# Reordering three transposes in an attention kernel: late queries, extra keys by way of the segment's key buffer, normed rows ahead of the extra keys

## Chip, cores and metric

One core of one Trainium2 chip. The metric is the device time of the core in microseconds (us), lower is better.

## What is computed

The input is 2048 tokens of 640 elements. `x` is normed and goes through attention in 64 segments of 32 tokens; each segment carries 8 memory rows that are the output of the segment before. So the segments are strictly one after the other. A ReLU-gated feed-forward block follows.

```python
# cut: B=1, S=2048, D=640, H=32 heads of 128, M=8 memory rows, seg=32, F=1728
def _A_ref(x, mem0, Wq, Wk, Wv, Wo, seg_len):
    mem = mem0
    for s in range(n_seg):
        xs = x[:, s * seg_len:(s + 1) * seg_len, :]
        h = jnp.concatenate([mem, xs], axis=1)          # 40 rows
        q, k, v = (einsum('btd,dhe->bhte', h, W) for W in (Wq, Wk, Wv))
        p = softmax(where(mask, q @ k.T * scale, -1e9))
        o = einsum('bhte,hed->btd', p @ v, Wo)
        mem = o[:, :M, :]
        outs.append(o[:, M:, :])
h  = x + _A_ref(layernorm(x), ...)
h2 = h + (relu(gate) * up) @ W_down                     # of layernorm(h)
```

## The kernel before

TensorE projects keys, then queries, then values. A segment's projection has 32 columns of room and only 8 memory rows, so 24 tokens of coming segments ride along ("riders"); every four segments the 32 tokens that are left over ("extra") are projected as filler work. I number the four kinds of segment by `s % 4`. Kind 2 does the extra keys and scales the normed rows of the next block; kind 3 follows it. In four later blocks (`EARLY`) kind 0 also scales rows, for the second norm.

Keys and queries must be transposed. They leave TensorE's output banks into four token buffers `tok` (0 and 1 keys, 2 and 3 queries). From there a DMA transpose, always issued by SyncE (SP), takes them to `KS` (keys), `QS` (queries) or, for the extra keys, straight to `Kr`. The normed rows go by the same queue from `xt` to `at`.

```python
    def dma_t(dst, src, r, w):
        add("sp", lambda e: e.dma_start_transpose(dst, src), r=r, w=w, dma=True)

    def trans_q(after=()):                       # QS <- tok[2], tok[3]
        dma_t(QS..., tokp[1][:, :], [("tok", 2), ("tok", 3)] + list(after), [("QS",)])
```

Every operation names what it reads (`r`) and writes (`w`). From these the program derives the waits: whoever overwrites a buffer waits until its readers are done. For a DMA "done" means landed. The wait stands in the queue of the engine that issues; SP works through its queue in order, so one wait of SP holds up all transposes behind it.

The loop, cut to what the change touches:

```python
        # ... keys of segment s projected into BQ
        dma_t(KS..., tokp[0][:, :], [("tok", 0), ("tok", 1)], [("KS",)])
        trans_ox()                               # oT <- ox, same queue
        # ... queries projected, copied to tok[2], tok[3]
        for f in late_k + late_q:
            f()
        qlate = nr and s % 4 < 2
        if nr and not qlate and s < NSEG - 2:
            trans_q()                            # kinds 2 and 3: at once
        loads()
        # ... values projected; pick_mem reads tok[2], tok[3] (L453)
        scores(s)                                # reads KS, Kr, Qr (L572)
        exp_mem()
        # ...
        if nr:
            v_riders(t0, nr, ...)                # small stores into Vr
            if s < NSEG - 2 and not qlate:
                evac_q(QS, ("QS",), t0, nr, M, "act")
        # ... filler work, memory values, mask
        n = n_rows(nb) if s % 4 == 2 and ln else 128 if e2b is not None else 0
        if n:
            row_scale(xt, ("xt",), n, xt, ("xt",))
        filler(4)
        if evac:
            evac()          # kind 2: tok[2], tok[3] <- BQ, then Kr <- tok
        # ... output projection
        if qlate and s < NSEG - 2:
            trans_q(...)                         # kinds 0 and 1: late
            late_k.append(... evac_q ...)
        pv_x(s, P0)                              # L690
        if n:
            dma_t(chunks_of(at[:, :])[:, :, 0:n], xt[0:n, :], [("xt",)], [("at",)])
```

The softmax here doesn't subtract the row's maximum and nothing guards it: scores larger than these inputs give would overflow.

## Time and profile before

| what | before |
|---|---|
| time | 1097.09 us, median of 3 runs (1093.23 to 1100.27) |
| span of the profiled run, granted clock | 1095.7 us, 0.997 |
| mean length of a segment, kinds 0, 1, 2, 3 | 13.28, 13.57, 13.67, 13.63 us |
| scores waiting for KS, all segments | 1.6 us in 5 waits |

A segment is measured from the end of the last product with the segment's own values (L690) to the end of the next one.

### The profile page before, as it was taken

How to read it: one execution, taken by the hardware profiler on the slowest of the kernel's cores; microseconds unless marked ns; L12 is line 12 of the kernel's file. 1: busy time of each engine (PE TensorE's matmuls, PEld its weight loads, DVE VectorE, ACT ScalarE, POOL GpSimd, SP SyncE). 2: the span in 40 equal slices, each digit the busy share in tenths (PEclk: the TensorE clock that was granted, in tenths of full speed). 3: DMA queues.
4: the chain of work that ended last, by engine and by line, in shares of the span. 5: the costliest groups of instructions: out<-in, count | busy, mean ns of one | idle time of the engine just before them, and what ended most of it. 6: DMA issues, size and time to landing. Idle time of an engine off the chain costs nothing.

```text
span 1095.7 us, 55782 instructions
## 1 busy us (share of the span) xinstructions
PE 1054.8 (96%) x27875; PEld 517.3 (47%) x23292; DVE 608.8 (56%) x1673; ACT 362.6 (33%) x792; POOL 260.0 (24%) x521
## 2 busy tenths in 40 slices
PE   4689999999999999999999999999999999999999
PEld 2344545454545454544454544454545465444444
DVE  3245656565656565666666666565656554553532
ACT  1214343333333333333333333333333322231211
POOL 1013232323223232323232323232323243000000
PEclk9999999999999999999999999999999999999999
DMA  9946464546454654556566666554555448122100
GB/s 363 387 101 106 89 107 90 102 89 104 90 98 95 102 94 97 94 114 108 112 113 112 110 109 109 100 97 95 95 94 93 92 118 288 45 78 74 29 19 25
DMA packets 285371, 121.61 MB, mean 111 GB/s; under 512 B 260880, under 2 KB 274788, under 8 KB 285136
## 3 DMA queue, kind: packets, MB, share of 16 engines
q1 hardware_dynamic: 267456, 95.52, 41.9%
q0 software_dynamic: 17264, 22.26, 8.8%
q8 instruction: 201, 3.29, 1.3%
q14 instruction: 34, 0.28, 0.1%
q10 hardware_dynamic: 416, 0.26, 0.1%
HBM read 36.79 MB, written 7.19 MB: 40 GB/s over the span
## 4 chain that ended last, share of the span: by engine, by line
PE 91%; DMA 5%; SPq 3%; DVE 1%; issue 1%; ACT 0%; DVEq 0%
PE ps L422 25%; PE ps L400 24%; PE ps L644 13%; PE ps L1051 11%; PE ps L690 3%; PE ps L666 3%; PE ps L572 3%; SPq L360 3%; DMA Wo<-in_A_Wo_dram 3%; PE ps L1092 3%; PE ps L609 2%; DMA KS<-tok 2%; PE ps L453 2%; PE ps L624 1%; DMA Kr<-tok 1%
## 5 line engine op out<-in xcount | busy, mean ns | idle before, releaser
L422 PE MATMUL ps<-W,act_r 128*32 128x512 bf16 x4292 | 406.5, 384 | 6.8 <-DMA W<-in_A_Wv_dram 2.6
L400 PE MATMUL ps<-W,act_r 128*32 128x512 bf16 x3588 | 362.4, 379 | 0.0
L422 PEld LDWEIGHTS ps<-W,act_r 128*32 128x32 bf16 x4292 | 132.1, 97 | 250.4 <-issue 151.3
L360 POOL DMA_DIRECT2D Vr<-Vp x312 | 156.1, 508 | 345.9 <-ACT Px L591 274.0
L464 ACT ACTIVATE tok<-ps 128x512 bf16<-128x512 f32 x192 | 110.9, 593 | 229.0 <-PE ps L400 200.2
L644 PE MATMUL ps<-Wo,oT 128*32 128x160 bf16 x8064 | 156.9, 234 | 8.7 <-DMA Wo<-in_A_Wo_dram 4.8
L466 DVE CAST tok<-ps 128x512 bf16<-128x512 f32 x131 | 90.6, 691 | 129.6 <-PE ps L400 109.8
L644 PEld LDWEIGHTS ps<-Wo,oT 128*32 128x32 bf16 x8064 | 142.8, 97 | 30.3 <-DVE oT L466 16.2
L422 PE MATMUL ps<-W,act_e 128*32 128x512 bf16 x900 | 89.3, 381 | 0.0
L400 PE MATMUL ps<-W,act_e 128*32 128x512 bf16 x900 | 88.9, 379 | 0.0
L555 DVE STREAM_TRANSPOSE TBf<-ps 128x64 f32<-128x64 f32 (+1 forms) x128 | 33.6, 263 | 95.8 <-PE ps L644 95.7
L360 POOL DMA_DIRECT2D attn_d<-wtok x62 | 46.4, 748 | 161.0 <-ACT wtok L464 161.0
L705 DVE TENSOR_TENSOR ox<-ps,rx 128x512 bf16<-128x512 f32 x128 | 82.5, 686 | 2.2
L464 ACT ACTIVATE Qr<-QS 128x512 bf16<-128x512 bf16 (+3 forms) x107 | 69.7, 680 | 35.9 <-DMA QS<-tok 35.9
L464 ACT ACTIVATE Vp<-ps 128x256 bf16<-128x256 f32 (+1 forms) x126 | 48.5, 385 | 81.5 <-PE ps L400 79.0
L1066 DVE TENSOR_TENSOR hT<-g,ps 128x512 bf16<-128x512 bf16 (+1 forms) x56 | 38.5, 688 | 47.2 <-PE ps L1051 43.4
L1051 PE MATMUL ps<-xn2T,Wg 128*128 128x512 bf16 x260 | 64.6, 379 | 0.0
L1051 PE MATMUL ps<-xn2T,Wu 128*128 128x512 bf16 x260 | 64.6, 379 | 0.0
L1064 ACT ACTIVATE g<-ps 128x512 bf16<-128x512 f32 (+1 forms) x56 | 32.4, 592 | 91.6 <-PE ps L1051 91.6
L466 DVE CAST Vp<-ps 128x512 bf16<-128x512 f32 x64 | 44.2, 691 | 28.4 <-PE ps L400 22.9
L464 ACT ACTIVATE wtok<-ps 128x160 bf16<-128x160 f32 x62 | 18.8, 303 | 117.0 <-DVE TBf L555 117.0
L1092 PE MATMUL ps<-Wd,hT 128*128 128x320 bf16 x210 | 57.2, 299 | 0.0
(121 smaller groups left out, 1190.7 us busy)
## 6 DMA issues: line engine op xcount, KB each, us to landing
Vr<-Vp POOLq DMA_DIRECT2D x124, 48.8 KB, 2.0
W<-in_A_Wk_dram SPq DMA_DIRECT2D x2, 2560.0 KB, 13.4
W<-in_A_Wq_dram SPq DMA_DIRECT2D x2, 2560.0 KB, 23.1
W<-in_A_Wv_dram SPq DMA_DIRECT2D x2, 2560.0 KB, 27.7
Wo<-in_A_Wo_dram SPq DMA_DIRECT2D x2, 2560.0 KB, 28.5
xt<-in_A_x_dram SPq DMA_DIRECT2D x30, 160.0 KB, 2.7
Vr<-Vp POOLq DMA_DIRECT2D x96, 32.5 KB, 2.1
at<-attn_d SPq DMA_DIRECT2D x16, 160.0 KB, 3.7
```

Of the source, the lines that this page charges most:

```text
L360: add(eng, lambda e: e.dma_start(dst, src), r=r, w=w, dma=True)
L400: return pe.add_instruction(mybir.InstMatmult(name=nc.get_next_instruction_name(), engine=mybir.EngineType.PE, ins=[pe.lower_ap(rhs), pe.l ...
L422: ins = pe.matmul(*a, start=(c == 0), stop=(c == DC - 1), skip_group_check=True)
L464: add("act", lambda a: a.activation(dst, src, ACTF.Copy), r=r, w=w)
L466: add("dve", lambda v: v.tensor_copy(dst, src), r=r, w=w)
L555: add("dve", lambda v, lo=lo, hi=hi: v.transpose(TBf[:, lo:hi, :].rearrange("p c t -> p (c t)"), src[:, 32 * lo:32 * hi]), r=[wkey], w=[(" ...
L572: i = pe.matmul(bank((P0, P1)[g % 2])[p:p + (M if a else 32), 40 * k:40 * k + 40], lh, Qr[:, h, q, :], start=True, stop=True, skip_group_c ...
L644: i = pe.matmul(bank(bk)[32 * gg:32 * gg + 32, 0:160], src[:, hb, :], w[:, gg], start=(hb == ORDER[0]), stop=(hb == ORDER[31]), skip_group ...
L705: add("dve", lambda v, kh=kh: v.tensor_tensor(ox[:, :, kh, :], src[:, :, kh, 0:128], ap(rx, kh, [[2, 4], [0, 128]]), ALU.mult), r=[B(b0 + ...
L1051: ins = pe.matmul(bank(bk), w[:, c, lo:lo + 128], xn2T[par][:, :, c, :], start=(c == 0), stop=(c == DC - 1))
L1066: add("dve", lambda v: v.tensor_tensor(hT[par][lo:128, j, :], g1[gi][lo:128, :], bank(bu)[lo:128, :], ALU.mult), r=[B(bu), ("g1", gi)], w= ...
L1092: i = pe.matmul(*a, start=(j == 0), stop=(j == FC - 1), skip_group_check=True)
```

## The change

Three parts, which I call A, B and C.

- **A, late queries:** in kind 2 the query transpose is issued after the memory mask, not right after the queries' copies, and its result is copied out in the next segment.
- **B, keys through KS:** the extra keys' tokens are copied into KS, which the scores have read by then, and Kr is transposed from KS. So `tok[2]` and `tok[3]` are free for the next segment at once.
- **C, rows first:** the normed rows' transpose is issued as soon as the rows are scaled, so that it stands ahead of Kr in SP's queue in kind 2, and ahead of the late query transpose in the four kind-0 segments.

```diff
@@ exp_mem @@                                                   # A
-                r=[("om",), ("mbd",)], w=[("Pbd", i)])
+                r=[("om",), ("mbd",)], w=[("Pbd", i), ("qgo", i)])
@@ extra_units / evac @@                                        # B
+                elif j == 1:
+                    copy_op(e, KS[:]...[:, 512 * i:512 * i + 512], bank(BQ[i]), [B(BQ[i])], [("KS",)])
                 else:
                     to_tok(BQ[i], 2 + i, e)
             if j == 1:
-                dma_t(Kr[q]..., tokp[1][:, :], [("tok", 2), ("tok", 3)], [("Kr", q)])
+                dma_t(Kr[q]..., KS[:]..., [("KS",)], [("Kr", q)])
@@ loop @@                                                      # A
-            if nr and not qlate and s < NSEG - 2:
+            qmid = nr and s % 4 == 2 and s < NSEG - 2
+            if nr and not qlate and not qmid and s < NSEG - 2:
                 trans_q()
@@                                                              # A
-                if s < NSEG - 2 and not qlate:
+                if qmid:
+                    trans_q([("qgo", 1)])
+                if s < NSEG - 2 and not qlate and not qmid:
                     evac_q(QS, ("QS",), t0, nr, M, "act")
@@                                                              # C
             row_scale(xt, ("xt",), n, xt, ("xt",))
+            dma_t(chunks_of(at[:, :])[:, :, 0:n], xt[0:n, :], [("xt",)], [("at",)])
@@                                                              # A
+            if s > 0 and qmid:
+                late_k.append(lambda t0=t0, nr=nr: evac_q(QS, ("QS",), t0, nr, M, "act"))
@@                                                              # C
         pv_x(s, P0)
         if n:
-            dma_t(chunks_of(at[:, :])[:, :, 0:n], xt[0:n, :], [("xt",)], [("at",)])
```

(Cuts: the views of KS and Kr are written as `...`.) No matrix product is added, removed or moved: TensorE's instructions stand in the same order in both kernels.

More of the change, by code (lines that the diff above doesn't have):

```diff
@@ L877, in evac @@
                     to_v(BQ[i], Vr[q], i, ("Vr", q), e)
+                elif j == 1:
+                    copy_op(e, KS[:].rearrange("p h t -> p (h t)")[:, 512 * i:512 * i + 512], bank(BQ[i]), [B(BQ[i])], [("KS",)])
                 else:
@@ L880, in evac @@
             if j == 1:
-                dma_t(Kr[q][:].rearrange("p h t -> p (h t)").rearrange("p (k r) -> p k r", r=128), tokp[1][:, :],
-                      [("tok", 2), ("tok", 3)], [("Kr", q)])
+                dma_t(Kr[q][:].rearrange("p h t -> p (h t)").rearrange("p (k r) -> p k r", r=128),
+                      KS[:].rearrange("p h t -> p (h t)"), [("KS",)], [("Kr", q)])
         def fin():
```

## The prediction

> **What bounds the kernel now.** I read the page first, then the waits, the stretches segment by segment, and last the queue of SyncE (SP) beside TensorE.
>
> From the page: busy time, then the chain that ended last.
>
> ```profile
> PE 1054.8 (96%) x27875; PEld 517.3 (47%) x23292; DVE 608.8 (56%) x1673; ACT 362.6 (33%) x792; POOL 260.0 (24%) x521
> ...
> PE 91%; DMA 5%; SPq 3%; DVE 1%; issue 1%; ACT 0%; DVEq 0%
> ```
>
> TensorE is occupied for 1054.8 of 1095.7 us. Of the missing 41 us, some 30 lie at the start, where the weights arrive (the chain has Wo<-in_A_Wo_dram and SPq L360 there). So the 63 segments between 60.8 and 908 us hold the whole prize of this change, and TensorE hardly stands still in them. The change touches no matrix product; it can only win what separates a disturbed segment from an undisturbed one.
>
> Next, the stretches, each from the end of one segment's last matmuls (L690) to the next one's. I call the four kinds of segment by their number modulo 4. Columns: length, then busy time per engine.
>
> ```profile
> 586.90:600.22 13.32, 13.32 (x414) 6.64 (x334) 9.40 (x27) 5.45 (x12) 2.73 (x5) 1.00 0.55 86
> 600.22:614.29 14.07, 13.68 (x438) 7.16 (x383) 8.07 (x25) 4.09 (x9) 2.74 (x5) 1.00 0.68 112
> 614.29:627.62 13.33, 13.33 (x422) 6.71 (x340) 8.98 (x27) 6.04 (x15) 5.92 (x11) 1.00 0.52 103
> 627.62:642.10 14.48, 13.54 (x420) 6.02 (x340) 7.62 (x22) 4.85 (x10) 4.26 (x10) 1.00 0.99 137
> ```
>
> These are kinds 0, 1, 2, 3. Over the whole loop kind 0 has a median of 13.23 us and kind 1 of 13.30 us, which I take as the undisturbed length of any kind. Summed over the loop (leaving out the second segment and the last full one, which have no filler work) the excess over 13.23 (13.30 in kind 1) is 0.8 us in kind 0, 3.2 in kind 1, 5.1 in kind 2, 6.0 in kind 3: about 15 us, 1.4% of the run. That is the ceiling.
>
> The queue of SP in the disturbed segments, and what TensorE says there:
>
> ```profile
> 601.46 1.29 SPq L363 DMA_TRANSPOSE at<-xt  x1
> 603.31 2.47 SPq L363 DMA_TRANSPOSE KS<-tok  x1
> ...
> 626.47 2.25 SPq L363 DMA_TRANSPOSE Kr<-tok  x1
> 629.17 1.21 SPq L363 DMA_TRANSPOSE at<-xt  x1
> 630.71 2.50 SPq L363 DMA_TRANSPOSE KS<-tok  x1
> ```
> ```profile
> 607.62 0.20 PE L572 MATMUL ps<-Qr,Kr 128*32 128x40 bf16 x4 [0.34 <-DMA KS<-tok]
> ...
> 633.84 0.36 PE L453 MATMUL ps<-ident,tok 128*128 128x32 bf16 x8 [0.87 <-DVE tok L466]
> ```
>
> The first pair: the normed rows' transpose (at<-xt) is issued 1.85 us ahead of the segment's keys (KS<-tok), whose issue then takes 2.47 us; undisturbed it takes 1.23 to 1.8. The keys land late and the scores (L572) stand 0.34 us. The second: VectorE could not overwrite tok because the extra keys' transpose (Kr<-tok) still read it, and TensorE stood 0.87 us. These are the two waits that the diff aims at. The landing times from the list of transfers:
>
> ```profile
> QS<-tok SPq DMA_TRANSPOSE x76, 3.1
> KS<-tok SPq DMA_TRANSPOSE x62, 3.2
> ...
> at<-xt SPq DMA_TRANSPOSE x19, 4.9
> Kr<-tok SPq DMA_TRANSPOSE x15, 5.2
> ```
>
> A transpose alone lands 3.1 us after its issue; at and Kr, issued back to back beside the value riders' stores, need 4.9 and 5.2.
>
> **What the Trainium skill says.** "DMA: Bandwidth & Descriptors", section "Issuing engines are not separate DMA queues": transfers started by different engines run on the same 16 DMA engines and interleave. The trace agrees, with those 5.2 us against 3.1. "Perfetto Trace Analysis", section "DMA Instruction — HWDGE (DVE, Sync)": what the profile shows of such a DMA begins when its semaphores are satisfied and ends when the sequencer is free; the movement lies outside. So 2.47 us for KS is issuing alone. This agrees with a landing (3.1) well beyond the issue (1.25). "Runtime: NRT & Kernel Launch", section "Instruction fetch mechanics": instructions are refilled in 16 KiB blocks of 256. Here the instruction queue q8 shows 201 packets and 3.29 MB, 16 KiB each, and TensorE has 51,167 recorded instructions, 200 blocks of 256. So these fetches share the DMA engines with the transposes, and a transfer that is moved can change stops that seem to have no releaser.
>
> **Part 1: normed rows first.** For kind 2 and four of kind 0, the at transpose is issued once VectorE has scaled the rows, not after the last matmuls are set up. In the kind-2 segment from 396.88 us, row scaling (L383) starts 11.28 us in and takes 0.44, so at can go out at 11.75; today Kr goes at 11.7 and at at 13.05 or, in about half the segments, 0.5 to 1.5 us into kind 3. In the four kind-0 segments scaling ends near 11.5, and at gets out ahead of the late query transpose at 13.2. That frees kind 1 of the pile-up: the four scores waits there are 0.16, 0.22, 0.35 and 0.56 us, 1.3 us in sum. The same four segments are 2.8 us too long in all; I count half of the rest as following from it. **Gain 2.0 us.**
>
> **Part 2: extra keys through KS.** The two ScalarE copies (0.6 us each) stay, only their target changes from tok to KS; no instruction is added. The tok wait vanishes: 0.87 us once, and about 0.5 us in the first kind-3 segment, which reached L453 at 5.79 us and not 5.28. **Gain 1.4 us.** The price: two new waits. The copies overwrite KS, which the scores have long read, but the graph also makes the store of the extra memory rows (attn_d<-at, 3.7 us to landing, issued at 7.0 and 7.6 us) a reader of KS, so the copies start near 11.3 us, not 10.55. Since at goes first in SP's queue until 13.0, this hides. Second, the next segment's KS transpose must wait until Kr has landed. Kr, issued near 13.0 and landing 4 us later, is done at 17.0, which is 3.5 us into kind 3, where KS is issued at 3.1 to 3.25 now. KS then issues fast, because at is no longer in front of it: 3.5 + 3.1 = 6.6 us, against scores at 6.9. Some segments will miss this by a few tenths. **Loss 1.0 us**: 14 segments, an average of 0.07.
>
> **Part 3: late queries in kind 2.** The QS transpose moves from 6.15 us to after the memory mask (L585), near 8.6 us, and its evacuation on ScalarE (0.63 + 0.40 us) to the next segment, after the token copy at 5.3 us: done at 6.3, with the scores at 6.9 and the next value copy at 7.2. So it just fits. It takes away QS traffic while exp and mask run: where QS landed at 9.2 us, the memory's value products (L609) started 1.05 us after the scores' last matmuls were issued; elsewhere, and in kinds 0 and 1, 0.92. That is 0.13 us in 12 segments, 1.5 us; I take 1.0, because the traffic is only moved, into the output projection (L644), where instruction fetches run. **Gain 1.0 us.**
>
> Sum: 2.0 + 1.4 - 1.0 + 1.0 = 3.4 us off 1097.1, which gives 1093.7.
>
> **Rivals.** (a) *The new KS wait takes the place of the tok wait.* If Kr lands at 18 us and not at 17, KS is issued 1.2 us late in all 14 kind-3 segments and the scores stand some 0.8 us each: 11 us lost, net 1105. For it: Kr is now second of two transposes and lands 5.2 us after issue today. Against it: the two together land at 16.7 to 17.5 us now in either order, and with QS gone from 6 us the memory rows' store should land sooner. (b) *The stops without a releaser move.* Kinds 2 and 3 lose up to 0.9 us in the output projection with no data wait, and kind 0 almost never. If they come from fetches behind transposes, three transposes in a row from 8.6 to 15 us may make each kind 2 longer by 0.3 us: 4.5 us lost, net 1098. Or taking at out of kind 3's beginning may remove them: some 5 us more won, net 1088. (c) *Nothing.* The waits that the diff removes sum to under 3 us of TensorE's time and everything else is hidden: 1095 to 1097.
>
> **Range and chances.** The three runs of before span 1093.2 to 1100.3, so plus or minus 3.5 us is noise between runs. With rival (b) both ways, 8 times in 10 the time should be between 1087.5 and 1100. Faster by over 2% needs 22 us, more than the ceiling of 15: 0.01. Slower by over 2% needs rival (a) at twice its size: 0.03. Within 2%: 0.96.
>
> **What would show each step.** Right: no KS wait over 0.1 us in kind 1; no wait of L453 for tok; kind 1's mean at 13.30; KS issued between 3.1 and 3.8 us in kind 3 and scores reached by 7.1; QS issued near 8.6 us in kind 2 with 0.92 us from the scores to L609. Wrong: KS in kind 3 issued after 4 us with the scores waiting for it (rival a), output projections of kind 2 longer than 2.5 us (rival b), or ScalarE's evacuation of QS holding up the scores in kind 3. The whole prediction falls if time moves outside the segment loop, which no part of the change touches.

## More of the kernel before

One view that the prediction does not show is the list of waits. Its columns: who waited `<-` for whom, us in total, number of waits, longest wait. For the scores in the kernel before it says:

```profile
PE ps L572 <- DMA KS<-tok: 1.6, 5, 0.6
```

So scores hardly ever wait for the keys' transpose.

## The result

| | before | after |
|---|---|---|
| median of 4 runs | 1095.91 us (1093.23 to 1100.27) | 1125.61 us (1120.17 to 1130.68) |
| span of the profiled run, granted clock | 1095.7 us, 0.997 | 1124.0 us, 0.992 |
| mean segment, kinds 0, 1, 2, 3 | 13.28, 13.57, 13.67, 13.63 us | 13.27, 13.79, 13.45, 15.53 us |

The changed kernel is slower: the ratio is 1.0266, 95% interval 1.0207 to 1.0326. All ratios here are the mean time of one kernel's fast runs over that of the other's of the same rounds, so not quite the ratio of the medians quoted.

**Where the time is.** The loop has 15, 16, 16 and 15 segments of the four kinds. From the traces, before rounding of the means: -0.2, +3.5, -3.4 and +28.6 us, +28.5 together. The spans differ by 28.3 us. So nothing outside the loop moved, and the loss is kind 3.

The changed kernel's page, busy time and the chain that ended last:

```profile
PE 1058.8 (94%) x27875; PEld 521.9 (46%) x23292; DVE 608.5 (54%) x1673; ACT 362.6 (32%) x792; POOL 259.3 (23%) x521
...
PE 84%; DMA 11%; SPq 3%; DVE 1%; issue 1%; ACT 0%; DVEq 0%
```

TensorE has the same number of instructions and 4.0 us more busy time. The chain moved: DMA has gone from 5% to 11% of it. Now the stretches of one block of four segments (same columns as in the prediction; the third number from the end is the granted clock):

```profile
605.39:618.76 13.37, 13.37 (x415) 6.15 (x334) 9.33 (x27) 5.45 (x12) 2.73 (x5) 1.00 0.62 103
618.76:633.42 14.66, 13.39 (x439) 7.25 (x383) 8.06 (x25) 4.09 (x9) 2.74 (x5) 1.00 0.54 99
633.42:646.89 13.47, 13.46 (x420) 6.68 (x340) 8.98 (x27) 5.33 (x13) 5.92 (x11) 1.00 0.55 107
646.89:664.20 17.31, 14.71 (x421) 6.77 (x340) 7.58 (x22) 5.56 (x12) 4.25 (x10) 0.90 0.58 107
```

Kind 3 (last row) lasted 17.31 us and TensorE was busy for 14.71 of them, although its products are the same as in the 13.54 us of before: it stood for 2.60 us, and a part of it then ran at a lower clock. Kind 1 (second row) stood for 1.27 us. TensorE in these two segments:

```profile
625.37 0.36 PE L453 MATMUL ps<-ident,tok 128*128 128x32 bf16 x8 [1.26 <-DVE tok L466]
...
656.55 0.20 PE L572 MATMUL ps<-Qr,Kr 128*32 128x40 bf16 x4 [2.60 <-DMA KS<-tok]
```

The 0.87 us wait of L453 for tok has left kind 3, as intended; instead the scores wait 2.60 us for KS, and a tok wait has turned up in kind 1. SP's queue says why:

```profile
616.95 1.21 SPq L363 DMA_TRANSPOSE at<-xt  x1
618.71 1.83 SPq L363 DMA_TRANSPOSE QS<-tok  x1
...
645.31 2.50 SPq L363 DMA_TRANSPOSE at<-xt  x1
647.86 1.31 SPq L363 DMA_TRANSPOSE Kr<-KS  x1
653.17 1.23 SPq L363 DMA_TRANSPOSE KS<-tok  x1
```

Between 647.86, when Kr starts to be issued, and 653.17 SP issues nothing. It waits for Kr to land, since the next transpose overwrites KS, which Kr reads. So KS is issued 6.28 us into kind 3 and not at 3.1. The waits, first TensorE's, then SP's own:

```profile
PE ps L572 <- DMA KS<-tok: 23.1, 15, 2.6
...
PE ps L453 <- DVE tok L466: 5.0, 4, 1.4
```
```profile
SPq L166 <- DMA Kr<-KS: 50.8, 15, 4.2
```

All 15 kind-3 segments wait for KS, 23.1 us in sum. The list of transfers (last number: median us from issue to landing) has the size that decides:

```profile
at<-xt SPq DMA_TRANSPOSE x19, 5.4
Kr<-KS SPq DMA_TRANSPOSE x15, 5.3
```

**The rest of kind 3.** 23.1 us less the 0.3 us of KS waits that kind 3 had before makes 22.8 of 28.6. The clock has most of the rest: four kind-3 segments, whose scores had stopped for 2.03, 2.44, 2.60 and 2.64 us, were each followed by a stretch of 3.4 us at a granted clock of 0.5 (beginning at 97.8, 210.4, 657.6 and 715.6 us). They lasted 17.3 to 17.5 us. A kind-3 segment with a stop of 2.39 us and no such stretch is this one:

```profile
311.92:327.81 15.89, 13.50 (x420) 6.52 (x340) 7.56 (x22) 5.56 (x12) 4.23 (x10) 1.00 0.53 92
```

Leaving out the stops, the four lasted some 1.2 to 1.7 us longer than this one, 5.8 us together. 22.8 + 5.8 is the 28.6 us, but this sum hides two shifts of 3.4 us that cancel: the output projections of kind 3 (L644, from the first product to the last) got shorter, 2.46 us on average and not 2.68, and smaller differences, mostly delays before the scores, took as much. The Trainium skill, "TensorE: Matmul & The Clock Gate", section "HAM oscillation — how this bites in real kernels", puts the rule as no idle gaps of TensorE over about 3.4 us. Here shorter stops sufficed, in four of the fifteen; the length of the slow stretch does agree with the page's 3.4 us.

Why 2.03 us sufficed and 2.39 us did not, the traces tell in part. The slow stretches of a run begin on a grid: in the changed kernel at 97.77, 210.41, 657.56, 715.59 and, in the last segment but one as before the change, 923.80 us, which are 33, 131, 17 and 61 times 3.413 us apart. In each of the four cases 2.03 us or more of the stop fell into the one cell of this grid before the slow stretch; the stop of 2.39 us lay across a boundary, with 1.97 us in one cell. So the place of a stop counts as well as its length. A limit does not follow: in lateq_undone (below) a cell with 2.01 us of stops was not followed by a slow one, and a cell with 1.78 us was.

**Kind 1.** The four kind-1 segments after a kind 0 that scales rows lost their KS waits (1.3 us in sum), as intended. But at now precedes the late query transpose. QS is issued about when kind 1 begins (618.71 above, kind 1 begins at 618.76) and lands 5.5 to 5.8 us into it, not at 3.1. VectorE may not overwrite tok until then: 5.0 us of tok waits. These four segments are 2.5 us longer in sum. The rest of kind 1's 3.5 us is no part of this: one segment (from 395.80 us) lasted 1.8 us longer, with a stop of 1.37 us for which the trace has no releaser, and the first one was 0.9 us shorter, because the run of before had a slow stretch there.

**Kind 2** won 3.4 us: the memory's value products (L609) start 0.93 us on average after the scores' last issue in place of 1.05, which is 1.8 us in 15 segments, and the output projections (L644) took 2.40 us on average in place of 2.52, which is the other 1.7 us. The late QS lands 14.6 to 16 us after kind 2 begins, and nobody waits for it.

### The profile page after: what moved, and what is told of

It is laid out like the page before. It is cut to its first block, busy times and chain, and to the rows that moved or that the text cites.

```text
span 1124.0 us, 55767 instructions
## 1 busy us (share of the span) xinstructions
PE 1058.8 (94%) x27875; PEld 521.9 (46%) x23292; DVE 608.5 (54%) x1673; ACT 362.6 (32%) x792; POOL 259.3 (23%) x521
## 4 chain that ended last, share of the span: by engine, by line
PE 84%; DMA 11%; SPq 3%; DVE 1%; issue 1%; ACT 0%; DVEq 0%
PE ps L422 23%; PE ps L400 21%; PE ps L644 13%; PE ps L1058 10%; DMA KS<-tok 4%; PE ps L666 3%; PE ps L572 3%; PE ps L690 3%; SPq L360 3%; PE ps L1099 3%; DMA Wo<-in_A_Wo_dram 3%; PE ps L609 2%; DMA QS<-tok 2%; DMA Kr<-KS 2%; PE ps L453 1%; PE ps L624 1%
## 5 line engine op out<-in xcount | busy, mean ns | idle before, releaser
L422 PEld LDWEIGHTS ps<-W,act_r 128*32 128x32 bf16 x4292 | 135.4, 97 | 249.9 <-issue 131.5
L464 ACT ACTIVATE tok<-ps 128x512 bf16<-128x512 f32 x162 | 94.6, 594 | 233.4 <-PE ps L400 196.8
L644 PE MATMUL ps<-Wo,oT 128*32 128x160 bf16 x8064 | 154.3, 234 | 6.0 <-DMA Wo<-in_A_Wo_dram 4.7
L644 PEld LDWEIGHTS ps<-Wo,oT 128*32 128x32 bf16 x8064 | 142.9, 97 | 25.0 <-DVE oT L466 16.2
L422 PE MATMUL ps<-W,act_e 128*32 128x512 bf16 x900 | 93.2, 397 | 0.0
L400 PE MATMUL ps<-W,act_e 128*32 128x512 bf16 x900 | 92.2, 393 | 0.0
L572 PE MATMUL ps<-Qr,Kr 128*32 128x40 bf16 x2048 | 41.4, 185 | 23.1 <-DMA KS<-tok 23.1
L572 PEld LDWEIGHTS ps<-Qr,Kr 128*32 128x32 bf16 x2048 | 39.0, 93 | 48.9 <-issue 48.6
L466 DVE CAST Vp<-ps 128x512 bf16<-128x512 f32 x64 | 44.3, 692 | 25.8 <-PE ps L400 19.7
```

Of the source, the lines that this page charges most:

```text
L400: return pe.add_instruction(mybir.InstMatmult(name=nc.get_next_instruction_name(), engine=mybir.EngineType.PE, ins=[pe.lower_ap(rhs), pe.l ...
L422: ins = pe.matmul(*a, start=(c == 0), stop=(c == DC - 1), skip_group_check=True)
L464: add("act", lambda a: a.activation(dst, src, ACTF.Copy), r=r, w=w)
L466: add("dve", lambda v: v.tensor_copy(dst, src), r=r, w=w)
L572: i = pe.matmul(bank((P0, P1)[g % 2])[p:p + (M if a else 32), 40 * k:40 * k + 40], lh, Qr[:, h, q, :], start=True, stop=True, skip_group_c ...
L644: i = pe.matmul(bank(bk)[32 * gg:32 * gg + 32, 0:160], src[:, hb, :], w[:, gg], start=(hb == ORDER[0]), stop=(hb == ORDER[31]), skip_group ...
```

## The experiments

My theory after reading: B makes the next KS transpose wait for Kr, and C puts Kr second in the queue, where it lands late; the two together make the 23 us. The rivals: the late queries (A) delay Kr by their traffic; the copies into KS, which wait for a store, delay it; or the new order in SP's queue costs by itself. Twelve kernels were run, in three groups of four; each group shares a chip and its runs of the kernel before (medians 1097.22, 1097.59 and 1100.27 us). All results were correct.

### Extra keys in a buffer of their own (own_buf)

All three parts, but the extra keys go through a buffer KX that nothing else in kind 3 uses (it shares its bytes with `oTn`, which is used in kind 1 only).

```diff
-    oTn = ar.alloc("oTn", [128, H, M], BF16)
+    KX = ar.alloc("KX", [128, H * SEG], BF16)
+    oTn = KX[:, 0:H * M].rearrange("p (h t) -> p h t", t=M)
-                    copy_op(e, KS[:]...[:, 512 * i:512 * i + 512], bank(BQ[i]), [B(BQ[i])], [("KS",)])
+                    copy_op(e, KX[:, 512 * i:512 * i + 512], bank(BQ[i]), [B(BQ[i])], [("oTn",)])
-                      KS[:].rearrange("p h t -> p (h t)"), [("KS",)], [("Kr", q)])
+                      KX[:, :], [("oTn",)], [("Kr", q)])
```

> Whole change, but the extra keys' tokens go to a buffer of their own, so that the next segment's KS transpose has nothing to wait for. Theory (the time is lost because KS transposes of kind-3 segments wait until Kr has landed, 5 us in): KS is issued at 3.1 to 3.3 us in kind 3, the 23.1 us of scores waiting for KS fall below 5 us, and the time falls to 1096 to 1104 us; the 5 us of kind-1 waits for tok stay. Rival (the transposes and stores themselves are backed up in the DMA engines, whatever SP waits for): KS is issued at 3.1 us but lands after 7.8 us behind Kr, scores still wait about 1 us in each kind 3, and the time stays at 1112 us or above.

Measured: 1101.09 us, ratio 1.0032 (1.0005 to 1.0058). SP's queue around a kind-3 segment that begins at 629.30 us, then the transfer's landing:

```profile
627.71 2.52 SPq L364 DMA_TRANSPOSE at<-xt  x1
630.28 1.31 SPq L364 DMA_TRANSPOSE Kr<-KX  x1
632.62 2.16 SPq L364 DMA_TRANSPOSE KS<-tok  x1
```
```profile
Kr<-KX SPq DMA_TRANSPOSE x15, 6.0
```
```profile
PE ps L573 <- DMA KS<-tok: 1.0, 5, 0.3
```

Kr lands even later after its issue, at 6.0 us, and it hurts hardly anybody: KS goes out 3.32 us into kind 3, the scores wait 1.0 us for KS in the whole run (last line; the scores are L573 here) and not 23.1, and the mean of kind 3 is 13.72 us. So the loss is not that Kr is late, but that KS has to wait for it. What is left over before is the tok waits (5.6 us, 5.2 of them in kind 1).

### B and C without the late queries (lateq_undone)

```diff
-            qmid = nr and s % 4 == 2 and s < NSEG - 2
-            if nr and not qlate and not qmid and s < NSEG - 2:
+            if nr and not qlate and s < NSEG - 2:
                 trans_q()
-                if qmid:
-                    trans_q([("qgo", 1)])
-                if s < NSEG - 2 and not qlate and not qmid:
+                if s < NSEG - 2 and not qlate:
```

> Change without the late queries: QS transposed at 6.1 us in kind 2 as before; keys through KS and rows first kept. If the late QS, colliding with the value riders' stores, is what delays at and Kr: QS lands at 9.2 us, Kr near 17 us (3.5 us into kind 3), KS issued at 3.5 us, time 1098 to 1106 us with the kind-1 waits for tok still there. If rows first is enough by itself to make Kr late: KS still issued at 5 us in kind 3, time 1112 us or above.

Measured: 1122.72 us, ratio 1.0241 (1.0205 to 1.0278). TensorE's wait:

```profile
PE ps L572 <- DMA KS<-tok: 23.1, 14, 2.5
```

The same 23.1 us without A. So the late queries are not needed for the loss.

### A and B, rows last as before (rows_undone)

```diff
             row_scale(xt, ("xt",), n, xt, ("xt",))
-            dma_t(chunks_of(at[:, :])[:, :, 0:n], xt[0:n, :], [("xt",)], [("at",)])
@@
         pv_x(s, P0)
         if n:
+            dma_t(chunks_of(at[:, :])[:, :, 0:n], xt[0:n, :], [("xt",)], [("at",)])
```

> Change without rows first: at goes after the last matmuls again; late queries and keys through KS kept. If at ahead of Kr is what makes Kr late: Kr issued near 12.5 us, lands by 17 us, KS in kind 3 issued by 3.7 us, and the kind-1 waits for tok (5 us) go back to the 1.3 us of KS waits: time 1096 to 1103 us. If the late QS is what makes it late: QS still lands at 14.6 us, Kr at 17.5 us or later, KS at 4.3 us or later in kind 3, time 1108 us or above.

Measured: 1100.01 us, ratio 1.0025 (0.9985 to 1.0066). TensorE's wait, SP's wait, and the landing:

```profile
PE ps L572 <- DMA KS<-tok: 1.8, 3, 0.7
```
```profile
SPq L166 <- DMA Kr<-KS: 15.4, 12, 1.8
```
```profile
Kr<-KS SPq DMA_TRANSPOSE x15, 4.5
```

With Kr first in the queue, SP still waits for it in 12 segments, but 15.4 us and not 50.8, and the reserve ahead of the scores covers nearly all of that. Kind 2 keeps its gain (13.39 us).

### A and C, extra keys through tok as before (keys_undone)

```diff
-                elif j == 1:
-                    copy_op(e, KS[:]...[:, 512 * i:512 * i + 512], bank(BQ[i]), [B(BQ[i])], [("KS",)])
                 else:
                     to_tok(BQ[i], 2 + i, e)
-                dma_t(Kr[q]..., KS[:]..., [("KS",)], [("Kr", q)])
+                dma_t(Kr[q]..., tokp[1][:, :], [("tok", 2), ("tok", 3)], [("Kr", q)])
```

> Change without the KS buffer: the extra keys' tokens go to tok again, which the late QS transpose still reads. Theory: the copies then wait until QS has landed (14.6 us, 1.4 us into kind 3) and hold TensorE's banks, so each kind 3 begins some 2 us late: 1125 to 1145 us, no better than the whole change. Rival (KS reuse is the only fault of the change): 1100 us or below.

Measured: 1163.2 us, ratio 1.0622 (1.057 to 1.0674). More than I expected; the direction was right, the size was not.

```profile
PE ps L422 <- ACT tok L464: 48.9, 15, 4.1
```

The extra keys' copies into tok must wait until the late QS, which reads tok, has landed; TensorE then waits up to 4.1 us for its output banks. These longer stops also brought the granted clock of the profiled run down to 0.977. So A cannot be had without taking the extra keys out of tok: B is A's precondition.

### Rows first alone (rows_only)

The kernel before with C's two hunks.

```diff
             row_scale(xt, ("xt",), n, xt, ("xt",))
+            dma_t(chunks_of(at[:, :])[:, :, 0:n], xt[0:n, :], [("xt",)], [("at",)])
@@
-            dma_t(chunks_of(at[:, :])[:, :, 0:n], xt[0:n, :], [("xt",)], [("at",)])
```

> Rows first alone, on the kernel before: the extra keys go through tok as before, QS is early. Theory now (at ahead of Kr is the cause; through which buffer Kr goes only decides who waits): Kr lands 4.8 to 6.1 us into kind 3, as it did without the late queries, so the token copies of kind 3, which would start at 4.7 us, wait some 0.5 to 1.2 us (11 us in sum), and kind 1 loses the 5 us for late QS: 1108 to 1118 us. Rival (rows first hurts only together with keys through KS): 1103 us or below.

Measured: 1109.57 us, ratio 1.0112 (1.006 to 1.0164).

```profile
PE ps L453 <- DVE tok L466: 14.4, 12, 2.1
DVE tok L466 <- DMA Kr<-tok: 20.8, 8, 3.4
```

Eight of the twelve waits, 8.4 us, are in kind 3: the same late landing of Kr, now felt through the buffer that Kr reads here, tok. The other four, 6.0 us, are in kind 1, where QS lands late behind kind 0's rows. C costs with either buffer.

### Keys through KS alone (keys_only)

The kernel before with B's hunks:

```diff
+                elif j == 1:
+                    copy_op(e, KS[:]...[:, 512 * i:512 * i + 512], bank(BQ[i]), [B(BQ[i])], [("KS",)])
-                dma_t(Kr[q]..., tokp[1][:, :], [("tok", 2), ("tok", 3)], [("Kr", q)])
+                dma_t(Kr[q]..., KS[:]..., [("KS",)], [("Kr", q)])
```

> Keys through KS alone, on the kernel before: QS early, at last. Theory: Kr is issued near 12 us and lands 3.3 to 4.1 us into kind 3, so KS is issued a few tenths late and lands at 6.5 to 7.3 us, about when the scores want it: 1094 to 1102 us. Rival (sharing KS is by itself what costs the 27 us): 1112 us or above, KS issued at 5 us.

Measured: 1095.51 us, ratio 0.9998 (0.9949 to 1.0047).

```profile
PE ps L572 <- DMA KS<-tok: 3.6, 9, 1.3
```
```profile
Kr<-KS SPq DMA_TRANSPOSE x15, 3.5
```

With Kr issued first and landing 3.5 us later, B gives and takes about the same. The copies into KS, which wait for the extra memory rows' store, are there in this kernel too and do no harm; they waited 9.1 us in sum here and 30.3 us in the changed kernel, but in rows_undone 26.6 us of such waits went with 1.0025. So that rival falls. The first rival has a little truth in it: with the late queries as well (rows_undone) Kr lands after 4.5 us and not 3.5, and SP waits 15.4 us for it and not 5.3; but no scores of kind 3 waited for KS there.

### Late queries alone (lateq_only)

The kernel before with A's hunks only (cut).

```diff
+            qmid = nr and s % 4 == 2 and s < NSEG - 2
+            if nr and not qlate and not qmid and s < NSEG - 2:
                 trans_q()
+                if qmid:
+                    trans_q([("qgo", 1)])
```

> Late queries alone, keys through tok, rows last: the copies of the extra keys into tok must wait for QS, which lands at 13 to 14 us, so that TensorE stands at the start of each kind 3 for some 2 us as it does with rows first: 1120 to 1140 us, a little less than the 1163 us of late queries with rows first because Kr no longer stands behind at. Rival (the late QS is cheap without rows first): 1105 us or below.

Measured: 1125.08 us, ratio 1.0233 (1.0187 to 1.0279); slower, though whether by 2% is open.

```profile
PE ps L422 <- ACT tok L464: 22.4, 14, 2.5
```

As in keys_undone, the extra keys' copies wait for the late QS and TensorE for its banks, but less.

### Rows first in kind 0 only, with A and B (rows_kind0)

```diff
             row_scale(xt, ("xt",), n, xt, ("xt",))
-            dma_t(chunks_of(at[:, :])[:, :, 0:n], xt[0:n, :], [("xt",)], [("at",)])
+            if s % 4 == 0:
+                dma_t(chunks_of(at[:, :])[:, :, 0:n], xt[0:n, :], [("xt",)], [("at",)])
@@
         if n:
+            if s % 4 == 2:
+                dma_t(chunks_of(at[:, :])[:, :, 0:n], xt[0:n, :], [("xt",)], [("at",)])
```

> The whole change, but rows first only in the four kind-0 segments. If kind 2's order is what makes KS late: the 23 us of waits for KS vanish and only the 5 us of kind-1 waits for tok are left: 1100 to 1107 us. If kind 0's rows matter more than thought: 1112 us or above.

Measured: 1104.88 us, ratio 1.0029 (0.9998 to 1.006).

```profile
PE ps L453 <- DVE tok L466: 4.9, 4, 1.8
```

The four tok waits of kind 1 are back (4.9 us; the changed kernel has 5.0), and the KS waits are down to 0.4 us. This puts the two costs of C apart: kind 0's is the tok waits, kind 2's the KS waits.

### Own buffer, late queries, rows first in kind 2 only (own_rows2)

```diff
# on top of own_buf
             row_scale(xt, ("xt",), n, xt, ("xt",))
-            dma_t(chunks_of(at[:, :])[:, :, 0:n], xt[0:n, :], [("xt",)], [("at",)])
+            if s % 4 == 2:
+                dma_t(chunks_of(at[:, :])[:, :, 0:n], xt[0:n, :], [("xt",)], [("at",)])
@@
         if n:
+            if s % 4 == 0:
+                dma_t(chunks_of(at[:, :])[:, :, 0:n], xt[0:n, :], [("xt",)], [("at",)])
```

> Whole change with a buffer of its own for the extra keys, and rows first only in kind 2; in the four kind-0 segments at goes after QS again. If rows first in kind 0 is what makes the four kind-1 segments wait 5.2 us for tok (QS lands at 5.8 us and not at 3.1): that wait vanishes, the 1.3 us of waits for KS come back, and the time falls by 3 to 4 us against the version with rows first in both: 1096 to 1099 us. If those waits come from something else, they stay and the time stays at 1100 to 1102 us.

Measured: 1092.79 us, ratio 0.9959 (0.9919 to 0.9999), kinds 13.34, 13.57, 13.30 and 13.58 us. Somewhat better than expected. It is the fastest version; against the kernel before its gain of 0.4% is at the edge of what these runs can tell.

### Own buffer, late queries, rows last as before (own_lateq)

```diff
# on top of own_buf
             row_scale(xt, ("xt",), n, xt, ("xt",))
-            dma_t(chunks_of(at[:, :])[:, :, 0:n], xt[0:n, :], [("xt",)], [("at",)])
@@
         if n:
+            dma_t(chunks_of(at[:, :])[:, :, 0:n], xt[0:n, :], [("xt",)], [("at",)])
```

> Own buffer and late queries, rows where the kernel before had them. What the first two parts are worth without the third: kind 2 at 13.3 us, kind 3 without waits for tok or KS but with at in front of KS: 1091 to 1097 us. It equals the version with rows first in kind 2 (1092.8) if the place of at makes no difference once nothing waits for Kr, and is 3 us or more slower if rows first is then a gain.

Measured: 1099.46 us, ratio 0.9989 (0.9953 to 1.0025). The time is above my range, on a chip whose runs of before are 3 us slower than I had assumed. The interval overlaps that of own_rows2, so these runs do not say whether rows first helps once the extra keys have their own buffer.

### Own buffer, rows' transpose in the next segment (own_rows_last, own_rows_last2)

If being second is what costs, could the rows be moved out of the pair altogether? First, behind the next segment's KS and oT transposes:

```diff
# on top of own_buf; the transpose after row_scale taken out
         if n:
+            late.append(lambda n=n: dma_t(chunks_of(at[:, :])[:, :, 0:n], xt[0:n, :], [("xt",)], [("at",)]))
```

> The opposite of the change's third part, with an own buffer for the extra keys and late queries: the rows' transpose goes last, after KS and the outputs' transpose of the next segment, where it lands near 8.7 us, still ahead of its readers. If the order of transposes is what decides: Kr goes out at 12 to 12.5 us, lands near 16, KS is issued at 3.1 us in all kinds and lands by 6.5, no scores wait over 0.1 us in kinds 1 and 3; 1088 to 1095 us, faster than both. If the stops of TensorE come from the amount of traffic and not its order: 1096 to 1102 us.

Measured: 1106.89 us, ratio 1.0106 (1.0041 to 1.0172). A miss.

```profile
PE ps L454 <- DVE tok L467: 9.6, 13, 1.3
```

The pair is apart: at lands 2.5 us after its issue, and the median of kind 3 falls to 13.28 us. But now the rows stand ahead of the next query transpose, which lands late: kind 0 waits for tok nine times (5.6 us), its mean rises to 13.99 us, and four kind-2 segments, which follow the transposes of kind 0's rows, wait 4.0 us. Second, behind the query transpose in kind 3, with kind 0's rows as before:

```diff
# on top of own_buf; the transpose after row_scale taken out
             if s % 4 == 2:
+                late_r.append(... dma_t(at <- xt) ...)
+                late_r.append(... ln1_back ...)
+            else:
+                dma_t(chunks_of(at[:, :])[:, :, 0:n], xt[0:n, :], [("xt",)], [("at",)])
@@                                          # after the next segment's trans_q()
+            for f in late_r:
+                f()
```

> Own buffer, late queries; kind 2's rows are transposed last of all in kind 3 (after KS, the outputs and QS), where the earlier try held QS back and made kind 0 wait; kind 0's rows go as in the kernel before. If order decides: kind 3 falls to 13.3 us as in that try, kind 0 is back at 13.25, kind 1 keeps its 1.3 us of waits: 1086 to 1092 us. If the waits in kind 0 came from something other than a late QS, kind 0 stays near 14 us: 1100 us or above.

Measured: 1111.5 us, ratio 1.009 (1.0063 to 1.0117). A second miss. SP's own wait, and TensorE's:

```profile
SPq L361 <- DMA at<-xt: 10.4, 4, 2.7
```
```profile
PE ps L454 <- DVE tok L467: 11.0, 4, 3.0
```

In the four EARLY blocks a load into at follows in kind 3 and has to wait in SP's queue until the rows' transpose has landed and been read; the queries behind it wait along, and kind 0 lasted 15.9 to 18.7 us there, in three of the four with a slow stretch of the clock as well. Elsewhere kind 0 was at 13.3 us. Kind 3 did not keep the 13.28 us of the first try: its median was 13.50. Both misses are the mechanism once more: whatever is moved hands its landing to the next one in the queue.

### The parts together

| parts | ratio to before | the wait that grew |
|---|---|---|
| B | 0.9998 | none of note |
| C | 1.0112 | tok: 8.4 us for Kr, 6.0 us for QS |
| A | 1.0233 | tok, for QS: 22.4 us |
| A + B | 1.0025 | none of note |
| B + C | 1.0241 | KS, for Kr: 23.1 us |
| A + C | 1.0622 | tok, for QS: 48.9 us |
| A + B + C (the change) | 1.0266 | KS, for Kr: 23.1 us |
| A + C, extra keys in own buffer | 1.0032 | tok, nearly all in kind 1: 5.6 us |

(Rows of different groups come from different chips, each against its own runs of before.) B cures A. C costs with any buffer that the next segment needs soon.

## Why the prediction was wrong

The prediction was 1093.7 us, with 3% for slower by over 2%; it came to 1125.61. Step by step:

- **What bounds the kernel: right.** TensorE in the loop, and no time moved outside it. The ceiling for a gain was right too; there was no such ceiling for a loss.
- **Part 2, the failed step: "Kr, issued near 13.0 and landing 4 us later, is done at 17.0 … Loss 1.0 us".** Both times are wrong. In 9 of the 15 segments at's issue took 2.2 to 2.6 us, not 1.2 (2.50 in the block shown), and Kr started up to 14.5 us into kind 2. And it landed 5.3 us after its issue. So it was done at 18.3 to 19.8, KS was issued 4.9 to 6.6 us into kind 3, and the loss was 22.8 us of waits and some 6 us of lower clock, in 15 segments and not 14. The right numbers stood in the prediction itself: of before it says that the second of the pair, then at, goes at 13.05 or 0.5 to 1.5 us into kind 3, and lands after 4.9 us. That is 18 to 19.7. The argument "the two together land at 16.7 to 17.5 us now in either order" took the landing of the first for that of the pair. Swapping two transfers swaps their landings: Kr, for which KS and with it the whole queue waits, was given the later one. The time from issue to landing hardly changed with the place (Kr 5.2 us as the first, 5.3 as the second; at 4.9 as the second, and 5.4 now); what Kr lost is its place in the queue, behind at's issue. own_buf (Kr late, SP not waiting for it) and rows_undone (Kr early, waiting all the same) show both halves.
- **Rival (a) was the right mechanism.** Its size of 11 us was worked out for a landing at 18, the earliest of those that happened, and without a change of clock.
- **Part 2, the gain of 1.4: in part.** The tok wait of 0.87 us is gone. The 0.5 us in the first kind-3 segment was not won: it reached L453 at 5.79 us again. The copies that wait for the memory rows' store (30.3 us in sum) ended 11.9 to 13.4 us into kind 2, hidden behind at's issue as predicted in 13 of 15 segments; in the other two they held up Kr by some 0.1 us.
- **Part 1, the gain of 2.0: wrong in sign.** The KS waits in kind 1 went, as predicted (1.3 us). But I had only asked what at stands in front of no longer, not what it stands in front of now: the late queries, whose landing costs 5.0 us of tok waits. The four segments lost 2.5 us. (A reading beside it was too narrow: the issue of an undisturbed KS took up to 2.1 us in the kernel before, not 1.8.)
- **Part 3, the gain of 1.0: right in mechanism, somewhat too small.** The 0.93 us from the scores to L609 is what was predicted, in 15 segments: 1.8 us. The other 1.7 us that kind 2 won belong to the next point.
- **Rival (b), moved stops: seen, on its favourable side.** No output projection of kind 2 grew. Those of kinds 2 and 3 got shorter, by 1.7 and 3.4 us in sum, which is the "some 5 us more won" that it named, hidden under the loss. That instruction fetches have to do with it is not shown; no run tests it.

**What stays open.** Why a transpose that is issued in the later part of kind 2 needs over 5 us, and not 3.1, I have only argued (the value riders' stores share the DMA engines); no run took the stores away. Standing behind another transpose is not needed for it: the late QS of the changed kernel, with no other transpose issued within 3 us of it, took 5.9 to 7.1 us, while in kind 1, behind no rows, QS took 3.1. One kind-1 segment of the changed kernel stood for 1.37 us with no releaser in the trace, and so did one in two of the experiments; I have no cause for it. And the gain of own_rows2 over the kernel before is small enough to be noise.

## What to carry to other kernels

When two transfers in one queue are swapped, the one that goes second gets the other's late landing: work out for both who waits for the landing, and take its time from the transfer that stands in that place now, its issue included. Lending a buffer that the next stage overwrites turns the borrower's landing into a wait of the issuing queue, and an in-order queue hands it to everything behind; a buffer of its own took nearly the whole of it away here (23.1 us of waits went to 1.0). And a stop of TensorE can cost more than its length, when the clock falls after it.

## What the Trainium skill lacked or had wrong

- "TensorE: Matmul & The Clock Gate", sections "Part 1: The HAM clock gate (the "warmup" mystery)" and "HAM oscillation — how this bites in real kernels": they speak of idle windows or gaps of about 3.4 us. In the changed kernel stops of 2.03, 2.44, 2.60 and 2.64 us were each followed by 3.4 us at a granted clock of 0.5, while one of 2.39 us, which lay across two cells of the grid of 3.413 us, was not.
- "DMA: Bandwidth & Descriptors", section "DMA Transpose (X-bar)", gives no time from issue to landing. Here a transpose landed 3.1 us after its issue at quiet times (the rows alone 2.5 us), and later in kind 2 some 5 to 7 us after it, be it as the second of two (Kr, 5.3) or by itself (the late QS, 6.1).
- The same page, section "Issuing engines are not separate DMA queues", says that the time to initiate a DMA "is usually small relative to the DMA itself". Here the issue of one transpose took 1.2 to 2.6 us against 3.1 us to landing, and held the queue of the issuing engine for as long.
